# One new list of steps for a delta rule and a multiplicative FFN on one core: loads on SyncE's queue, clearing in steps of its own, and copies that name their engine

## The chip, the cores and the metric

The kernel runs on one core of a Trainium2 chip. The metric is device microseconds of one execution; lower is better. TensorE (PE) multiplies, VectorE (DVE), ScalarE (ACT) and GpSimd (POOL) work on vectors, and SyncE (SP) issues transfers. Each engine takes its instructions in order.

## The reference

```python
# deltanet: B, H, S, D = 4, 8, 768, 48
k_n = k / (norm(k, axis=-1) + 1e-06)
state = zeros((B, H, D, D))
for t in range(S):
    y[:, :, t] = einsum('bhd,bhde->bhe', q[:, :, t], state)
    v_old = einsum('bhde,bhd->bhe', state, k_n[:, :, t])
    state += beta[:, :, t] * outer(k_n[:, :, t], v[:, :, t] - v_old)
# multiplicative FFN on x = y as (3072, 384); d_ff = 1024
out = (((x @ w1) * (x @ w2)) @ w3) @ w_out
```

The queries, keys, values and beta are float32; the weights come as float64, so the kernel makes float32 of them.

## The kernel before

The sequence is cut into 12 chunks of 64 tokens, and the recurrence is brought to matrix products per chunk, with the inverse of a triangular matrix for each batch, head and chunk. Two chunks make a pair: `V0` is the inverse for chunks 0 and 1, and so on to `V5`. The FFN is folded: `w3 @ w_out` is made once (`w34`, eight folds), so that the FFN is `((x @ w1) * (x @ w2)) @ w34`. From the second pair of chunks on, the large products are done with fewer multiplications and sums on the vector engines.

The order of the whole program is written out in a string, `ORDER`, of step names. Every name stands for a Python generator; each time the name comes up, the generator runs to its next `yield`, and what it issues goes to the queues of the engines. At the end every engine is held to this order. The names that matter here:

- `P0` to `P7` are pieces of w_out, `P8` to `P23` of w3, `P24` to `P35` of w1 and w2. A piece (`piece`) has four steps: its transfer into one of five buffers `raw` (SP), two passes on ACT (L799, L802), a shift of bits on DVE (L804), and a sum on POOL (L806), which frees the buffer. The sixth transfer waits for the first sum.
- `k`, `q`, `v` and `p` load keys, queries, values, and keys and queries in another layout (`perm`, `spare`). `k0` and `q0` are issued from ACT's queue, the others from SP's.
- `K0`, `Q0`, `K1`, `Q1` (`by_tensor`, L352) turn the keys and queries of the first two chunks on PE; four copies follow, two of the keys' on DVE (L364), the others on ACT (L362). `d2` and on turn them on DVE instead (L339).
- `t0` to `t15` turn pieces of w3 on PE (L841), with a copy on ACT (L844). Piece P(8 + n) belongs to t(n). `f0` to `f7` are the folds (L855), in two halves, with a copy on ACT (L862).
- `g` makes squares of the keys (POOL, L285) and their sums (DVE, L287), and copies them across partitions (ACT, L274 and L276). `N` makes the norms of a pair in 15 small instructions of DVE, and copies across again.
- `s` is the scores of a chunk (PE, L383 and L389), with U made on DVE (L395) and P copied on ACT and masked on POOL. `u` copies U into columns (ACT, POOL, ACT).
- `V` is the inverse: POOL clears its start, DVE turns the columns (L466), ACT copies the start into PSUM (L475), 31 steps of two DVE instructions follow (L484, L489), and DVE turns the result back (L503). For the pairs from the third on, transfers take the place of some copies.
- `e` is the corner of the inverse for a chunk: copies from the result (ACT, POOL, ACT), a turning on DVE (L559), and two rounds of products on PE (L576) with copies on ACT.
- `c` is the chain through the state (L647), `y` the output of a chunk (L746). `a`, `b`, `h`, `i`, `j` are the FFN's first products (L875, L994), `S` and `G` sums for them, `o` and `x` the last products (L1104) and the results.

Before the first step, `padded` lets POOL clear `TT`, `perm`, `spare`, `x_room`, the ends of the four key tiles, and four more tiles (L198).

Of the kernel before, what the change touches and what calls it, by code (L numbers as in the profile page):

```python
# [39 lines left out]
V0 P0 k0 beta P18 P13 P0 P18 P0 P0 P11 g0 P13 K0 P18 K0 P11 P18 P10 P13 P13 q0 P3 P3 P11 g0 beta  # L40
beta K0 K0 K0 k1 K1 P10 P11 P12 P3 P12 g0 g0 Q0 P10 g0 g0 g0 g0 g0 P8 Q0 Q0 Q0 K1 K1 K1 Q0 K1 P3
N0 P9 k2 P8 P8 P10 s0 P8 N0 g1 s0 s0 s0 s0 s0 s0 u0 q1 P2 Q1 P9 p2 P2 P12 P12 P9 Q1 g1 Q1 Q1 P2
u0 g1 Q1 d2 d2 u0 P5 P1 t0 t0 t5 t5 P9 t2 t2 P4 P6 s1 s1 P5 P5 P2 s1 P1 s1 s1 s1 u1 g1 P1 u1 u1
t4 V0 V0 P5 V0 V0 P4 t10 P7 P4 t3 t3 V0 V0 P1 f1 P6 P6 t4 V0 P7 V0 V0 t10 t1 P14 P7 P4 V0 f0 V0
P6 P16 P16 V0 V0 P7 t1 s0 P19 P19 P19 P19 V0 f1 P17 k3 p2 v1 V0 V0 P14 P14 P14 V0 f2 P17 f2 f0 V0
f2 P15 v0 P20 f1 t11 f0 P17 P17 f5 V0 V0 P16 t11 P16 t8 P15 V1 V0 t8 f5 t9 V0 V0 t6 P15 V0 n0 n0
f5 V0 V0 V0 V0 t9 P20 P20 V0 t6 P22 P22 P22 f4 P23 P23 V0 f4 f4 P21 P21 P15 t7 t7 V0 s1 V0 V0 V0
V0 g1 d2 d2 P22 f3 f3 P24 P20 g1 g1 p3 g1 P26 p3 P30 e0 e0 e0 t12 t14 e1 e1 g1 f3 e0 e0 d3 d3 N1
s2 s2 s2 P23 P23 t12 e0 f6 e0 p4 s2 P24 e1 e1 t14 s2 e0 P24 s2 P25 c0 P26 f7 u2 P30 P24 c0 e1 e1
P21 P21 d3 d3 y0 y0 P26 P26 P31 t15 t13 s3 s3 s3 s3 s3 s3 t13 c0 n1 n1 P32 t15 u2 u2 u3 c0 P30 f7  # L50
e1 P25 P25 P31 P31 P27 c1 c1 u3 u3 f6 e1 c1 V1 V1 V1 y0 P31 f6 f7 P25 P27 V1 V1 V1 V1 P30 b1 c1
N1 b1 v2 P32 V1 V1 P27 V1 s1 y1 y1 b2 V1 d4 V1 V1 P28 P29 P32 b2 P27 V2 V1 V1 V1 y1 b3 V1 V1 P28
P28 b0 P32 c1 b2 b2 b3 b1 b1 b0 P29 P29 b0 P29 a03 a03 a02 V1 b0 V1 d4 V1 V1 a01 V1 P28 V1 V1 a02
V1 P35 a01 a00 a00 n2 n2 a04 a04 b7 P33 P33 a05 a05 P34 P34 a01 a07 b7 V1 b4 b5 V1 V1 V1 V1 k4
a01 a07 k5 b5 b3 g2 b4 V1 V1 P35 V1 V1 g2 c1 e2 e2 e2 e2 a06 a06 g2 e3 e3 e3 b3 g2 g2 a00 a02 a02
p4 v3 d4 d4 p5 a00 e2 P34 c2 c2 e2 P34 e2 b6 P35 P35 e2 c2 c2 e3 a03 g2 g2 P33 b6 y2 g2 P33 g2 d5
d5 p5 c2 c2 y2 a04 e3 s4 N2 e3 s4 a03 s4 b6 b6 s4 s4 s4 s4 T e3 T T d5 n3 d5 a04 e3 b4 b4 b7 s5
n3 k6 g3 u4 s5 s5 s5 s5 s5 s5 b5 b7 b5 a05 T c3 c3 a06 a05 a06 u5 V2 p6 g3 a07 a07 c3 c3 g3 S0 S0
S0 V2 g3 V2 V2 N2 oD0 y3 y3 V2 V2 W oA0 S0 S0 V2 V2 S0 S0 S0 c3 v5 n5 V2 V2 S0 S0 S0 S0 V2 v4 oB0
V2 V2 V2 xA0 V2 V2 xB0 V2 V2 oA0 S0 S0 S0 n4 oB0 xA0 d6 y3 k7 xA0 V2 n4 oC0 V2 V2 V2 a10 xB0 S0  # L60
V2 V2 xC0 G1 V2 xD0 a10 a10 V2 oC0 a10 a10 d6 xC0 xC0 xC0 xD0 V2 V2 i10 V2 h10 c3 c4 V2 V2 j10 V2
V2 V2 a10 h10 i10 a12 V2 V2 h10 W W a12 p6 V2 a12 a12 j12 e4 g3 g3 h10 c4 a12 h10 a12 h12 d6 d6
s5 i12 e4 e4 e4 i10 h12 h12 g3 g3 p7 g3 e4 e4 h12 N3 s4 h12 a11 a11 a11 s6 s6 i12 i12 e5 c4 j11
s6 c4 y4 y4 c4 e5 d7 d7 h11 c4 c5 a11 p7 e5 s6 a11 a11 h11 i11 i11 n5 c5 d7 d7 N3 a13 h11 h11 e5
W e5 s7 e5 a13 s7 s7 s7 s7 s7 s7 a13 a13 s6 s6 c5 i11 k8 u7 u6 g4 g4 g4 S1 V3 V3 c5 p8 h11 s6 g4
h13 a13 j13 a13 i13 h13 i13 i13 S1 h13 V3 h13 h13 V3 V3 y5 V3 V3 V3 V3 V3 V3 d8 V3 V3 V3 y5 oC1
oA1 S1 oD1 S1 S1 V3 V3 S1 xA1 c5 oA1 xA1 oB1 v6 y5 v7 a20 a20 V3 xA1 V3 V3 V3 d8 G2 V3 V3 xB1 n6
V3 V3 V3 V3 oB1 xB1 xC1 S1 j20 k9 V3 xD1 V3 V3 V3 V3 S1 oC1 a20 a20 p8 xC1 V3 xC1 h20 V3 xD1 xC1
# [27 lines left out]
def kernel(  # L96
# [13 lines left out]
    B, H, S, D = q.shape  # L110
    P = 128
# [65 lines left out]


# [15 lines left out]
    def padded(name, shape, n, start=0):  # L194
        res = []
        for i in range(n):
            t = persist.tile(shape, FP32, name=f"{name}{i}")
            pool.memset(t[:, start:] if start else t[:], 0.0)  # L198
# [146 lines left out]
    def by_tensor(m, i, src):  # L345
        KQ = KQs[m] if m in KQs else new_KQ(m)
        ps = [bank([P, NR, NP, C]) for z in range(2)]
        for r in range(NR):
            for h in range(H):
                for z in range(2):  # L350
                    x = half(z if i else (z + h) % 2)
                    pe.matmul(  # L352
                        ps[z][feat(h % 2), r, h // 2, :], lhsT=src[x, r, h, :],
                        rhs=ident[x, x], start=True, stop=True,
                    )
        yield
        for z in range(2):
            for e in range(2):
                o = KQ[feat(e), NR * z : NR * z + NR, :, i, :].rearrange("p b a t -> p (b a) t")
                x = ps[z][feat(e)].rearrange("p r a t -> p (r a) t")  # L360
                if i or e:
                    act.copy(out=o, in_=x)  # L362
                else:
                    dve.tensor_copy(out=o, in_=x)  # L364
                yield
# [471 lines left out]
    def transpose_w3(jc, hf):  # L837
        ps = bank([P, 4, P])
        w3 = w3s.pop((jc, hf))
# [4 lines left out]
        act.copy(out=w3Ts[jc, hf][:], in_=ps[:].rearrange("p a b -> p (a b)"))  # L844
# [4 lines left out]
    def fold(jc):  # L849
        ps = bank([P, CW])  # L850
        first = not folded
# [10 lines left out]
        act.copy(out=w34[:, jc, :], in_=ps[:, 0:DM])  # L862
# [352 lines left out]
    for m in range(2):  # L1215
        parts[f"q{m}"] = lambda m=m: load_q(m, act.dma_start if m == 0 else sync.dma_start)
# [77 lines left out]
```

## Time and profile before

| | us |
|---|---|
| Median of 3 runs | 555.05 (553.54 to 555.67) |
| Profiled execution, its own time | 554.45 |
| Profiled execution, span | 552.7 |
| PE busy in the span | 521.4 |
| DVE, ACT, POOL busy | 362.1, 187.6, 253.6 |
| Mean granted clock of PE | 0.994 |

A row of a timeline has its start and the time it lasted in us, the engine, the line of the kernel, the operation, out<-in, and the count; in brackets stands the idle time ahead of it and what ended that. SPq and ACTq are the queues in which an engine issues transfers. A row of waits has the engine and line that waited, what it waited for, the total in us, how often, and the longest.

### The profile page before, as it was taken

The numbers are of one execution on the slowest core, as the hardware profiler recorded it, in microseconds if no ns is written. First come the engines' busy times: TensorE is split into PE (matmuls) and PEld (weight loads), VectorE is DVE, ScalarE is ACT, GpSimd is POOL, SyncE is SP. The second block draws the span as 40 slices with busy tenths as digits, with TensorE's granted clock in tenths as the row PEclk, the third lists the DMA queues.
The fourth block names the chain that finished last, engine by engine and source line by source line (L and its number), as shares of the span: only waits on it lengthen the run. The fifth ranks groups of instructions, "written<-read, shape, count | busy, mean of one in ns | idle before, by whom it ended". The sixth has DMA issues, their size and how long they took to land.

```text
span 552.7 us, 19818 instructions
## 1 busy us (share of the span) xinstructions
PE 521.4 (94%) x8540; PEld 447.8 (81%) x8540; DVE 362.1 (66%) x814; ACT 187.6 (34%) x393; POOL 253.6 (46%) x278
## 2 busy tenths in 40 slices
PE   3686999999999999999999999999999999999997
PEld 2563666688878988889987889988899888998897
DVE  2757877798767878569967579858587654123332
ACT  4788388955633012422022430123231121300000
POOL 8466555453569960365343255510492212342141
PEclk9997999999999999999999999999999999999999
DMA  8987987669356345454553564253601220020001
GB/s 251 203 223 189 199 188 141 120 159 150 55 90 127 80 106 80 61 101 81 114 98 61 79 121 86 86 83 43 125 16 44 62 51 5 9 66 1 0 1 57
DMA packets 197687, 52.64 MB, mean 95 GB/s; under 512 B 185344, under 2 KB 191488, under 8 KB 197600
## 3 DMA queue, kind: packets, MB, share of 16 engines
q1 hardware_dynamic: 193408, 50.59, 44.6%
q10 hardware_dynamic: 4192, 0.79, 0.9%
q8 instruction: 67, 1.10, 0.8%
q14 instruction: 20, 0.16, 0.1%
HBM read 41.25 MB, written 8.91 MB: 91 GB/s over the span
## 4 chain that ended last, share of the span: by engine, by line
PE 80%; DMA 6%; ACT 5%; DVE 4%; SPq 2%; issue 1%; DVEq 0%; ACTq 0%
PE ps_f L994 33%; PE ps_f L1104 19%; PE ps_f L855 7%; PE ps_w L647 6%; PE ps_f L875 6%; PE ps_w L746 4%; PE ps_w L576 2%; DMA X<-in_q_dram 2%; PE ps_w L383 2%; PE ps_w L389 1%; DMA raw<-in_moe_w_dram 1%; DMA ktok<-in_k_dram 1%; SPq L253 1%; DVE KQ L339 1%; ACT raw L802 1%
## 5 line engine op out<-in xcount | busy, mean ns | idle before, releaser
L1002 DVE TENSOR_TENSOR ab<-ab,ps_f 128x512 f32<-128x512 f32 x80 | 54.5, 682 | 57.3 <-PE ps_f L994 56.8
L1075 POOL TENSOR_TENSOR ab<-ab 128x512 f32<-128x512 f32 (+1 forms) x56 | 61.3, 1116 | 41.8 <-PE ps_f L1104 25.4
L994 PE MATMUL ps_f<-xT,w1s 128*128 128x256 f32 x320 | 78.5, 382 | 0.0
L1041 POOL TENSOR_TENSOR ab<-ab,late 128x512 f32<-128x512 f32 x19 | 24.1, 1271 | 107.0 <-DVE ab L1002 106.3
L994 PEld LDWEIGHTS ps_f<-xT,w1s 128*128 128x128 f32 x320 | 59.9, 190 | 7.9
L1104 PE MATMUL ps_f<-w,ab 128*128 128x192 f32 x376 | 65.5, 328 | 0.0
L1104 PEld LDWEIGHTS ps_f<-w,ab 128*128 128x128 f32 x376 | 61.3, 190 | 1.3 <-issue 0.5
L409 POOL TENSOR_TENSOR PT<-PT,smask 128x512 f32<-128x512 f32 x20 | 25.5, 1277 | 54.9 <-ACT PT L407 54.9
L855 PE MATMUL ps_f<-w2s,w3T 128*128 128x384 f32 x128 | 45.9, 510 | 4.9 <-ACT w3T L844 4.9
L1104 PE MATMUL ps_f<-room,ab 128*128 128x192 f32 x272 | 47.2, 328 | 0.0
L500 DVE TENSOR_TENSOR ps_w<-ps_w,tb 128x31 f32<-128x31 f32 (+15 forms) x124 | 43.3, 349 | 4.2
L767 ACT COPY xT<-ps_w 48x256 f32<-48x256 f32 x96 | 30.4, 365 | 44.8 <-PE ps_w L746 44.3
L1104 PEld LDWEIGHTS ps_f<-room,ab 128*128 128x128 f32 x272 | 44.3, 190 | 0.6 <-issue 0.3
L495 DVE TENSOR_TENSOR tb<-ps_w,Ub 128x31 f32<-128x31 f32 (+15 forms) x124 | 41.9, 338 | 3.6 <-ACT ps_w L475 0.3
L1010 ACT COPY ab<-ps_f 128x512 f32<-128x512 f32 x20 | 11.7, 586 | 95.1 <-PE ps_f L994 95.0
L994 PE MATMUL ps_f<-xT,room 128*128 128x256 f32 x160 | 41.3, 385 | 0.3 <-DVE ab L1002 0.2
L855 PEld LDWEIGHTS ps_f<-w2s,w3T 128*128 128x128 f32 x128 | 24.4, 198 | 20.8 <-issue 6.6
L994 PE MATMUL ps_f<-xT,w2s 128*128 128x256 f32 x160 | 40.1, 381 | 0.0
L994 PE MATMUL ps_f<-x_room,w2s 128*128 128x256 f32 x160 | 38.9, 386 | 0.0
L994 PEld LDWEIGHTS ps_f<-xT,room 128*128 128x128 f32 x160 | 29.5, 190 | 5.5 <-DVE ab L1002 1.1
L994 PEld LDWEIGHTS ps_f<-x_room,w2s 128*128 128x128 f32 x160 | 29.5, 190 | 5.1 <-DVE late L1002 1.0
L994 PEld LDWEIGHTS ps_f<-xT,w2s 128*128 128x128 f32 x160 | 30.1, 190 | 4.0
(143 smaller groups left out, 977.2 us busy)
## 6 DMA issues: line engine op xcount, KB each, us to landing
raw<-in_moe_w_dram SPq DMA_DIRECT2D x16, 512.0 KB, 6.7
vtok<-in_v_dram SPq DMA_DIRECT2D x24, 192.0 KB, 4.4
raw<-in_moe_w_dram SPq DMA_DIRECT2D x24, 192.0 KB, 4.9
out_dram<-osb SPq DMA_DIRECT2D x46, 96.0 KB, 1.7
ktok<-in_k_dram SPq DMA_DIRECT2D x44, 96.0 KB, 3.4
raw<-in_moe_w_out_dram SPq DMA_DIRECT2D x8, 384.0 KB, 4.5
perm<-in_k_dram SPq DMA_DIRECT2D x40, 64.0 KB, 2.8
perm<-in_q_dram SPq DMA_DIRECT2D x32, 64.0 KB, 2.8
```

Source lines behind the costliest of these rows:

```text
L409: pool.tensor_tensor(out=PT, in0=PT, in1=smask[:].unsqueeze(1).to_broadcast([P, H, C]), op=ALU.mult)
L495: dve.tensor_tensor(out=tv, in0=V[:, 0 : s + 1, s : s + 1].to_broadcast([P, s + 1, n]), in1=U[:, s, s + 1 : BS].unsqueeze(1).to_broadcast( ...
L500: dve.tensor_tensor(out=o, in0=o, in1=tv, op=ALU.subtract)
L647: pe.matmul(out(ps, r, h, z), lhsT=lhs(r, h, z), rhs=rhs(r, h, z), start=True, stop=True,)
L767: act.copy(out=xT[f, p:NP:2, b : b + NR, cc, :].rearrange("p a r t -> p r a t"), in_=pyv[f, z, b : b + NR],)
L855: pe.matmul(ps[:, 0:DM], lhsT=w3Ts[jc, kc // 4][:, kc % 4 * P : kc % 4 * P + P], rhs=wo[:, kc], start=(i == 0), stop=(i == KF - 1),)
L875: pe.matmul(ps[:].rearrange("p b c t -> p b (c t)"), lhsT=w[:, m, js], rhs=x[:, m, :, c0:c1].rearrange("p b c t -> p b (c t)"), start=(m = ...
L994: pe.matmul(acc[name][:, n * i : n * i + n], lhsT=ws[b][:, P * i : P * i + P], rhs=xs[x], start=new and k == 0 and i == 0, stop=k == len(t ...
L1002: dve.tensor_tensor(out=o_, in0=x, in1=acc[name], op=ALU.add)
L1041: eng.tensor_tensor(out=Z1, in0=Z1, in1=late, op=ALU.mult)
L1075: pool.tensor_tensor(out=o_, in0=x_, in1=y_, op=op)
L1104: pe.matmul(ps[b][:, b, :], lhsT=block(u, HF * f + i, z)[:, P * b : P * b + P], rhs=ws_[w][:, i], start=first and i == 0 and (b == 0 or n ...
```

## The change

1. `k0` and `q0` are issued from SP's queue, as the other loads are.
2. `padded` only notes what is to be cleared. Two new steps clear: `zd` on DVE (half of `TT`, those half columns of `perm` and `spare` that the loads leave out), and `zp` on POOL (the rest), one tile each time the name comes up.
3. A mark `'` behind a step's name swaps the engine of the copy that it issues: with it, a copy that was ACT's is DVE's and the other way. It holds for the copies of `K`, `Q`, `t` and `f`. A number behind `+` lets a step issue products that nobody reads; the list has none.
4. `ORDER` is a new list. It names the same steps, with the three novelties, in another order throughout.

In the new list, the first transfers are P12, P10, k0, q0, P11, beta, k1, P8, P18, P0, P13, q1; in the old one they are P0, k0 (ACT), beta, P18, P13, P11, P10, q0 (ACT), P3, k1.

```diff
 ORDER = """
-V0 P0 k0 beta P18 P13 P0 P18 P0 P0 P11 g0 P13 K0 P18 K0 P11 P18 P10 P13 P13 q0 P3 P3 P11 g0 beta
-beta K0 K0 K0 k1 K1 P10 P11 P12 P3 P12 g0 g0 Q0 P10 g0 g0 g0 g0 g0 P8 Q0 Q0 Q0 K1 K1 K1 Q0 K1 P3
...
-f5 V0 V0 V0 V0 t9 P20 P20 V0 t6 P22 P22 P22 f4 P23 P23 V0 f4 f4 P21 P21 P15 t7 t7 V0 s1 V0 V0 V0
-V0 g1 d2 d2 P22 f3 f3 P24 P20 g1 g1 p3 g1 P26 p3 P30 e0 e0 e0 t12 t14 e1 e1 g1 f3 e0 e0 d3 d3 N1
...
+P12 zp zp zp P10 P10 P12 zd P12 P12 P10 k0 K0 g0 g0 K0' g0 q0 V0 P10 K0' Q0 Q0' K0' zd P11 beta k1
+beta K0 P11 beta g0 P8 Q0' Q0 Q0 P8 g0 P11 g0 zp g0 g0 K1 P8 P18 P11 K1 g0 K1 K1' K1 P18 N0 P0 P0
+P13 t3 P8 s0 P0 P18 P0 P18 zp q1 P5 P9 k2 t2 P13 s0 s0 t2 P13 Q1 P5 zd Q1' Q1 t3 P3 P2 P13 s0 s0 s0
+s0 u0 u0 Q1' Q1' P5 p2 t4 P9 u0 P3 P7 P5 g1 t4' P9 P9 s1 P1 s1 s1 s1 s1 s1 u1 u1 u1 t0 t0' P3 t1 P2
+g1 t5 P2 P3 P2 V0 V0 V0 V0 P7 t1 d2 V0 P1 t5 P6 P7 P6 V0 d2 P1 t10 P7 t10 P4 P16 V0 V0 V0 V0 P6 V0
...
+g1 f4 P15 t7 t6 t7 f3 f3 v1 v0 N1 P21 e1 e0 P22 e0 n0 e0 e0 e0 d2 s2 P23 p3 e1 P29 P21 P21 e0 s2 t14
...
 """
...
+    def put(eng, out, in_):
+
+        on_act = (eng is act) != bool(other)
+        (act.copy if on_act else dve.tensor_copy)(out=out, in_=in_)
...
+    zeros = []
+
+    def padded(name, shape, n, start=0, where=None, eng=pool):
...
-            pool.memset(t[:, start:] if start else t[:], 0.0)
+            zeros.append((eng, where(t) if where else t[:, start:] if start else t[:]))
...
+    def zero(part):
+        for eng, t in zeros:
+            if (eng is dve) == part:
+                eng.memset(t, 0.0)
+                yield
...
-                if i or e:
-                    act.copy(out=o, in_=x)
-                else:
-                    dve.tensor_copy(out=o, in_=x)
+                put(act if i or e else dve, o, x)
...
+    parts["zd"] = lambda: zero(True)
+    parts["zp"] = lambda: zero(False)
...
-        parts[f"k{m}"] = lambda m=m: load_k(m, act.dma_start if m == 0 else sync.dma_start)
+        parts[f"k{m}"] = lambda m=m: load_k(m)
...
-        parts[f"q{m}"] = lambda m=m: load_q(m, act.dma_start if m == 0 else sync.dma_start)
+        parts[f"q{m}"] = lambda m=m: load_q(m)
...
     def step(name):
 
+        name, _, n = name.partition("+")
+        other[:] = name[len(name.rstrip("'")):]
+        name = name.rstrip("'")
+        unread[0] = int(n or 0)
```

More of the change, by code (lines that the diff above doesn't have):

```diff
@@ L51 @@
[L51 to L56, printed above, removed]
@@ new lines @@
+oC1 oA1 V3 V3 V3 V3 V3 V3 V3 V3 S1 S1 n6 s6 xA1 y5 p8 oB1 oD1 V3 V3 V3 V3 S1 S1 oA1 n6 s7 V3 V3 V3
+xB1 V3 V3 V3 k8 V3 V3 y5 oB1 d8 xA1 y5 V3 d8 V3 V3 G2 xA1 xB1 V3 V3 xC1 c5 a20 a20 k9 xC1 a20 j20 V3
+v7 V3 V3 a20 V3 xD1 S1 S1 oC1 xC1 p8 V3 V3 n7 a20 a20 V3 V3 V3 V3 V3 h20 h20 i20 c5 e6 h20 h20 i20
+a22 a22 a22 h20 a22 h22 a22 a22 i22 i20 xD1 a21 d8 e6 e6 h22 c6 h22 g4 g4 d8 e6 e6 N3 e6 c6 h22 j22
+xC1 e7 a21 a21 g4 g4 g4 g4 e7 i22 i22 g4 c6 e7 a21 a21 a21 c6 h21 y6 p9 e7 c6 j21 h22 h21 d9 g4 d9
@@ new lines @@
+c6 y6 n7 V4 g4 N4 v8 n8 i21 h21 p9 s8 h21 s8 s8 s8 s8 s8 s8 i21 a23 a23 a23 c7 u8 d9 d9 p10 a23 s9
+i23 h21 c7 s9 s9 s9 s9 s9 s9 i21 s9 u9 V4 e7 j23 a23 h23 a23 h23 V4 e7 V4 c7 c7 h23 y7 h23 i23 i23
+h23 S2 S2 y7 V4 V4 V4 V4 V4 V4 V4 d10 V4 V4 oD2 oA2 c7 d10 xA2 oA2 xA2 S2 S2 V4 S2 V4 V4 V4 s8 V4 V4
+V4 S2 S2 oB2 xB2 y7 V4 oC2 oB2 V4 c7 V4 xB2 xC2 G3 v9 S2 n8 a30 a30 a30 V4 xA2 k10 V4 oC2 j30 xD2
+k11 xC2 xD2 a30 V4 V4 xC2 a30 V4 V4 V4 V4 V4 a30 h30 h30 xC2 i30 n9 V4 V4 V4 V4 V4 a32 h30 c8 p10
@@ L92 @@
+c11 c11 xB4 c11 y10 oD4 y10 y11 y11 y11 oA4 S4 S4 S4 S4 oB4 oC4 xB4 xD4 xC4 a50 xC4 xD4 G5 oC4 a50
+a50 a50 xA4 j50 xA4 xC4 xC4 h50 a50 i50 a50 h50 i50 h50 h50 a52 a52 a52 h52 i50 h50 a52 a52 a52 h52
+j52 h52 h52 i52 i52 a51 a51 a51 h51 i52 h52 a51 a51 a51 h51 j51 h51 h51 h51 i51 i51 i51 a53 a53 a53
+a53 h53 a53 j53 a53 h53 h53 h53 h53 i53 i53 i53 S5 S5 o5 x5 o5 o5 S5 o5 x5 x5 S5 o5 x5 S5 S5 o5 x5
+x5 x5 S5 x5 x5 x5 S5 o5 x5 x5 x5 x5
 """
@@ L176, with fill @@
     pe, dve, act, pool, sync = nc.tensor, nc.vector, nc.scalar, nc.gpsimd, nc.sync
+    other = []
+    unread = [0]
+    def fill(ps):
+        for _ in range(unread[0]):
+            pe.matmul(
+                ps, lhsT=ident[:], rhs=ident[:].unsqueeze(1).to_broadcast([P, 4, P]),
+                start=True, stop=True,
+            )
+    def put(eng, out, in_):
+        on_act = (eng is act) != bool(other)
+        (act.copy if on_act else dve.tensor_copy)(out=out, in_=in_)
     small.tile([P, 40], FP32, tag="pad", name="pad", bufs=1)
@@ L191 @@
         pool.tensor_copy(out=smask[half(z), :], in_=strict[half(z), half(z)])
-    def padded(name, shape, n, start=0):
+    zeros = []
+    def padded(name, shape, n, start=0, where=None, eng=pool):
         res = []
@@ L197, in padded @@
             t = persist.tile(shape, FP32, name=f"{name}{i}")
-            pool.memset(t[:, start:] if start else t[:], 0.0)
+            zeros.append((eng, where(t) if where else t[:, start:] if start else t[:]))
             res.append(t)
         return res
-    TTx = padded("TT", [P, 2, NR, H, C], 1)[0]
-    TTs = [TTx[:, i] for i in range(2)]
-    perm = padded("perm", [P, B, NP, 2, BS], 1)[0]
-    spare, x_room = (padded(x, [P, n], 1)[0] for x, n in (("spare", 1024), ("x_room", 512)))
+    def zero(part):
[3 more added lines that the diff above has]
+                yield
+    TTx = padded("TT", [P, 2, NR, H, C], 1, where=lambda t: t[:, :, :, :, 0:BS], eng=dve)[0]
+    TTs = [TTx[:, i] for i in range(2)]
+    perm = padded(
+        "perm", [P, B, NP, 2, BS], 1, where=lambda t: t[:, :, :, :, D - BS :], eng=dve
+    )[0]
+    spare = padded(
+        "spare", [P, 1024], 1, eng=dve,
+        where=lambda t: t[:].rearrange("p (g d) -> p g d", d=BS)[:, :, D - BS :],
+    )[0]
+    x_room = padded("x_room", [P, 512], 1)[0]
     def perms(m):
@@ L347, in by_tensor @@
         ps = [bank([P, NR, NP, C]) for z in range(2)]
+        fill(ps[0].rearrange("p r a t -> p (r a t)"))
         for r in range(NR):
@@ L377, in scores @@
             ps = two_banks()
+            fill(ps[:, 0])
             for h in range(H):
@@ L838, in transpose_w3 @@
         ps = bank([P, 4, P])
+        fill(ps[:].rearrange("p x f -> p (x f)"))
         w3 = w3s.pop((jc, hf))
@@ L843, in transpose_w3 @@
         w3Ts[jc, hf] = slab("w3T")
-        act.copy(out=w3Ts[jc, hf][:], in_=ps[:].rearrange("p a b -> p (a b)"))
+        put(act, w3Ts[jc, hf][:], ps[:].rearrange("p a b -> p (a b)"))
         yield
@@ L850, in fold @@
         ps = bank([P, CW])
+        fill(ps[:])
         first = not folded
@@ L861, in fold @@
         yield
-        act.copy(out=w34[:, jc, :], in_=ps[:, 0:DM])
+        put(act, w34[:, jc, :], ps[:, 0:DM])
         yield
```

72 lines of the change are left out of this document (30 added, 42 removed).

## The prediction

> **What bounds the kernel now.** I read the page first, then the stretches, then who waits for whom on TensorE (PE), then the queues of the opening in order of time.
>
> ```profile
> span 552.7 us, 19818 instructions
> PE 521.4 (94%) x8540; PEld 447.8 (81%) x8540; DVE 362.1 (66%) x814; ACT 187.6 (34%) x393; POOL 253.6 (46%) x278
> ```
>
> PE is busy for 521.4 of 552.7 us, so only 31.3 us can be had without taking matmuls away. The stretches (columns: window, length, busy time of PE, weight loads, DVE, ACT, POOL; clock; DMA share; GB/s) say where they lie:
>
> ```profile
> 0.00:48.50 48.50, 26.19 (x496) 21.15 (x496) 26.40 (x60) 35.27 (x64) 33.68 (x48) 0.96 0.83 214
> 48.50:81.60 33.10, 33.09 (x116) 20.37 (x116) 25.41 (x66) 20.05 (x37) 18.30 (x19) 0.95 0.90 204
> 81.60:540.00 458.40, 453.19 (x7876) 397.57 (x7875) 307.22 (x683) 132.27 (x293) 200.75 (x211) 1.00 0.40 76
> 540.00:552.70 12.70, 8.98 (x56) 8.68 (x54) 3.12 (x7) 0.00 (x0) 0.88 (x1) 1.00 0.19 62
> ```
>
> 22.3 us of PE's idle time lie ahead of 48.5, none in the next 33 us, 5.2 in the long middle, 3.7 at the end. The change can win in the opening; behind it, it can mostly lose. PE's waits in the opening:
>
> ```profile
> PE ps_f L352 <- DMA ktok<-in_k_dram: 12.4, 4, 4.7
> PE ps_f L855 <- ACT w3T L844: 4.9, 2, 4.7
> ```
>
> First it waits for keys, later for a copy on ScalarE (ACT). The fold (L855) needs all of w_out (pieces P0 to P7), and each piece takes two passes on ACT, one on DVE, one on POOL. After the folds PE meets the corner of the first inverse (L576), which needs the 31 steps on VectorE:
>
> ```profile
> 45.86 1.62 PE L855 MATMUL ps_f<-w2s,w3T 128*128 128x384 f32 x2 [4.67 <-ACT w3T L844]
> 48.51 14.67 PE L855 MATMUL ps_f<-w2s,w3T 128*128 128x384 f32 x40 [0.18 <-ACT w3T L844]
> 63.46 2.75 PE L855 MATMUL ps_f<-w2s,w3T 128*128 128x384 f32 x8
> ...
> 80.69 1.04 PE L841 MATMUL ps_f<-ident,w 128*128 128x128 f32 x8
> 81.66 0.74 PE L576 MATMUL ps_w<-T,U 33*33 33x32 f32 x63
> ```
>
> So 81.66 is the time to forecast: the order on PE is almost the same work before and after that corner in both lists, and what follows is dense.
>
> **The change part by part.**
>
> *Keys and queries on SyncE (SP).* The issues of k0 and q0 leave ACT's queue; SP now sends two w3 pieces (1.05 MB), then k0, q0, a third piece, beta, k1.
>
> ```profile
> 8.42 2.47 PE L352 MATMUL ps_f<-ident,ktok 64*48 64x64 f32 x62 [3.27 <-DMA ktok<-in_k_dram]
> 10.74 2.71 SPq L225 DMA_DIRECT2D ktok<-in_k_dram  x4
> 18.55 1.83 PE L352 MATMUL ps_f<-ident,ktok 64*48 64x64 f32 x57 [1.04 <-DMA ktok<-in_k_dram]
> ```
>
> k0 was all there at 8.42. I put it at 8.5: about as many bytes stand ahead of it (one w_out piece, beta and the first w3 piece then, two w3 pieces now). Bounds: 7.5, and 11.9 if the 1.05 MB go wholly first (the rival below). k1 waits for SP's earlier transfers and goes out from about 8.2 on; from issue to the last block of its turning took 18.55 - 10.74 = 7.8 us, so 16.0 instead of 18.55. q1 is sent behind a piece that waits for POOL's second sum, at about 15.3 (the old list sends it behind k2); its copies come late enough in ACT's queue not to hold it. ACT wins the time of issuing, but it would only have waited for its first piece then: worth 0.
>
> *Clearing in own steps.* POOL cleared everything ahead of its first sum:
>
> ```profile
> 2.51 1.80 POOL L198 MEMSET TT<- 128x2048 f32 x1
> 9.32 1.02 POOL L806 TENSOR_TENSOR w2s<-w2s,raw 128x384 uint32<-128x384 uint32 x1
> 18.72 1.61 POOL L285 TENSOR_TENSOR sq<-ktok 128x384 f32<-128x384 f32 x2 [2.15 <-DVE w L804]
> ```
>
> Now it clears x_room and two pads first and sums from about 9.2, when the first piece has been through ACT: no gain there. DVE clears half of TT while it has nothing else (0 on the path, at most 1.80), and a quarter of that area twice more, ahead of beta's copy and of the second query's (0.2 to 0.9 each; ACT has 2 us queued beside them). Taken as 0.
>
> *ACT's queue, up to the first inverse.* 16.0, the squares of k1 (1.61), one reduction (0.54, a group below) and 0.1 give the crossing copies of the norms at 18.3 instead of 21.66.
>
> ```profile
> 21.66 0.19 ACT L274 COPY ss<-ss 128x16 f32<-128x16 f32 x1
> 25.69 0.67 ACT L799 ACTIVATE w<-raw 128x512 f32<-128x512 f32 x1
> 26.82 0.19 ACT L274 COPY wt<-wt 128x16 f32<-128x16 f32 x1
> 40.84 2.15 ACT L446 COPY columns<-U 96x512 f32<-96x512 f32 x2
> 43.02 1.21 ACT L475 COPY ps_w<-Vb 128x512 f32<-128x512 f32 x2
> 46.97 0.58 ACT L799 ACTIVATE w2s<-raw 128x384 f32<-128x384 f32 x1
> 47.87 0.59 ACT L844 COPY w3T<-ps_f 128x512 f32<-128x512 f32 x1
> ```
>
> Prices: a copy 0.6 (half of 1.21), a w3 piece 1.15 (25.69 to 26.82), a w_out piece 0.95 (46.97 to 47.87), a columns copy 1.07. From the crossing (0.6) to the end of the copies into V (1.21) ACT had 2 w3 and 3 w_out pieces, 10 copies of keys and queries, 3 of w3, 3 masks, 4 columns and a crossing of weights (0.6): 21.5, and took 22.6 (21.66 to 44.23). Now it has 3 and 4 pieces, 4 copies of keys and queries, 2 of w3, 3 masks, 4 columns: 3.45 + 3.8 + 5.4 + 4.3 with the two ends 1.8, or 18.7. With 1.0 for waits the copies into V end at 38.0 instead of 44.23. The copies that DVE takes over (0.67 each, the group below) lie beside this: DVE is busy 26.40 of 48.5 us. What would be late next is P2 or the columns on POOL, both some 1 us ahead of their use.
>
> *The first inverse.* DVE's groups between 44.4 and 75.6 (count, busy, mean ns, idle before), and three groups of the opening:
>
> ```profile
> L489 DVE TENSOR_TENSOR ps_w<-ps_w,tb 128x31 f32<-128x31 f32 (+15 forms) x31 | 10.8, 349 | 1.1
> L484 DVE TENSOR_TENSOR tb<-ps_w,Ub 128x31 f32<-128x31 f32 (+15 forms) x31 | 10.5, 339 | 0.8
> L804 DVE TENSOR_SCALAR w<-w 128x512 uint32<-128x512 uint32 x7 | 3.0, 422 | 5.3 <-ACT w L799 5.3
> L804 DVE TENSOR_SCALAR w2s<-w2s 128x384 uint32<-128x384 uint32 x3 | 1.1, 357 | 0.0
> ...
> L364 DVE COPY KQ<-ps_f 48x512 f32<-48x512 f32 x4 | 2.6, 674 | 1.6 <-PE ps_f L352 1.6
> L287 DVE TENSOR_REDUCE ss<-sq 128x8 f32<-128x384 f32 x6 | 3.3, 544 | 1.2 <-POOL sq L285 1.2
> L339 DVE STREAM_TRANSPOSE KQ<-perm 128x512 f32<-128x512 f32 x2 | 1.3, 690 | 2.8 <-DMA perm<-in_k_dram 2.8
> ...
> 75.68 1.25 DVE L503 STREAM_TRANSPOSE Ub<-ps_w 128x1024 f32<-128x1024 f32 x1
> 79.92 0.71 DVE L559 STREAM_TRANSPOSE T<-TT 128x512 f32<-128x512 f32 x1 [0.91 <-ACT TT L549]
> 81.74 0.14 DVE L294 TENSOR_SCALAR seed<-ss 128x32 uint32<-128x32 uint32 x1
> 85.01 0.19 DVE L318 TENSOR_TENSOR wt<-wt,beta_tok 128x32 f32<-128x32 f32 x1
> ```
>
> From the copies' end (44.23) to the turning back (75.68) are 31.4 us: 5.3 of waiting for ACT's weights, 26.1 of steps and ten shifts of pieces. The new list has ten shifts there too, and besides three turnings of keys or queries (0.69) and three reductions (0.54): 3.7. With 1.2 of waiting: 38.0 + 26.1 + 3.7 + 1.2 = 69.0 instead of 75.68.
>
> *The corner, where the list loses.* From the turning back (75.68) to the turning of the corner (79.92) passed 4.2 us, taken by copies on ACT and POOL. The new list has the norms of the second pair (81.74 to 85.20, 3.5 us of DVE) and a shift ahead of that turning; they fill the 3.0 us in which DVE waited and cost 0.9 more. 69.0 + 4.2 + 0.9 = 74.1, turned (0.71) at 74.8, and half a microsecond to PE: 75.3 instead of 81.66, **-6.4**.
>
> *Is PE there by then?* ACT has four w_out pieces (3.8) and three copies of w3 (1.8) after 38.0, and POOL sums the last (1.02): 44.6 for all of w_out. Nine half folds of 2.6 (row 63.46, 8 matmuls) and six turnings of w3 (0.48, half of 80.69 to 81.66) bring 70.9, and the slow clock at their start, as in the 14.67 for five halves, 1.7 more. So PE comes at 72.6 and waits 2.7 us for the corner, perhaps longer, and that may cost clock:
>
> ```profile
> 44.00:45.00 1.00, 0.00 (x0) 0.88 0.35 82
> 45.00:51.00 6.00, 4.96 (x10) 0.50 0.89 294
> 51.00:52.00 1.00, 1.00 (x3) 0.71 1.05 315
> ```
>
> The clock fell to half in the fourth microsecond of the wait that began at 41.2 and came back 5.7 us after PE began again: at most 2.9 us lost. The Trainium skill, "TensorE: Matmul & The Clock Gate" (What's actually happening), says that an idle window of about 3.4 us halves the clock, which this agrees with. By that rule a wait of 2.7 us would keep the clock, and the sum would be 1.0 less. I take a third of the loss, **+1.0**, since the wait is less sure than its distance from the fourth microsecond; bounds 0 and 2.9.
>
> *The rest.* V1, V2 and so on are spread over DVE much as before, and the end on PE is the same. New are pairs with little between: the second chain step follows the first's state with only one block of scores between them. **+0.5** from the 5.2 us of idle middle; bounds -3 and +5.
>
> Sum against the profiled execution's own 554.45 (span 552.7 and 1.75 around it): 554.45 - 6.4 + 1.0 + 0.5 = 549.55. The median of the runs shown, 555.05, is 0.6 above that execution; I give **550.0**.
>
> **The rivals.** *One ring.* k0 goes behind 1.05 MB, which at the 294 to 315 GB/s above take 3.4 us: 11.9, and keys, squares, columns and V0 all come 3.4 later, 553.4, no change. The Trainium skill, "DMA: Bandwidth & Descriptors" (Issuing engines are not separate DMA queues; Queues, rings and completion order), speaks against this change: SP and ACT each have a ring on the same engines, served in turn, and each ring starts in its order. For it: the 1.05 MB now stand ahead on k0's own ring. Against: with a ring to itself k0's last part came only at 8.42, after PE had stood 3.27 us for it, so sharing had already cost it most of this.
>
> *The inverse waits for weights* (slower). In the new list six w3 shifts stand inside V0, and ACT's passes for them stand behind copies that wait for folds on PE. The old inverse stood four times, 5.3 in all; if each of the six stands for 1.8, that is 10.8 instead of 1.2: 559.6. It decides from 9 us in all (550.0 + 7.8 passes the old time by 0.5%). For it: DMA is 0.90 busy in 48.5 to 81.6, and the old inverse did stand. Against: by the sum above ACT is through with w_out 4 us sooner.
>
> *More than that.* No clock lost, PE's 5.2 us of idle middle cut by 3: 545.2.
>
> That the copies do not move can be left out: the changed program's queues have them where the list says.
>
> **How the numbers follow.** Forecast 0.46 (547 to 552.2), more 0.14, one ring 0.19, slower 0.21. About 0.5%, 2.8 us, is what a measurement of this kernel can tell: faster 0.60, same 0.19, slower 0.21. The range leaves out the lowest tenth and half of the slower case: 544 to 559.
>
> **What would show it.** Right: PE's first L352 at about 8.5; ACT's copies into V ending near 38; 31 steps from 38 to 69; corner on PE near 75 with a wait of about 3 us for DVE. Wrong: k0 near 12; shifts in V0 with waits of over 1.5 each; a fold that waits for w_out past 47; or more than 8 us of idle PE from the corner to 540.

## The result, and the profile after

| | before | after |
|---|---|---|
| Median, us | 554.88 (553.54 to 555.67) | 568.55 (566.89 to 570.31) |
| Profiled execution, span | 552.7 | 567.4 |
| PE busy in the span | 521.4 | 526.2 |
| First corner on PE begins at | 81.66 | 79.47 |
| From there to the end | 471.0 | 487.9 |

The new kernel is slower: ratio 1.0249, 95% interval 1.0211 to 1.0288. The forecast of 550.0 was wrong by 18.6 us. Single executions fall now and then into a slower state of the chip; ratios leave these out, medians do not, so the two can differ a little.

The page of the new kernel, and its stretches with the cuts at its own corner (columns as before):

```profile
span 567.4 us, 19834 instructions
PE 526.2 (93%) x8540; PEld 450.0 (79%) x8540; DVE 369.6 (65%) x825; ACT 183.3 (32%) x385; POOL 251.3 (44%) x275
```

```profile
0.00:48.50 48.50, 30.96 (x514) 23.81 (x514) 31.70 (x74) 34.60 (x61) 30.31 (x42) 0.82 0.90 226
48.50:79.50 31.00, 26.01 (x100) 15.68 (x99) 29.25 (x73) 15.74 (x29) 15.95 (x19) 1.00 0.91 199
79.50:554.70 475.20, 460.32 (x7879) 401.88 (x7880) 305.50 (x673) 132.94 (x295) 204.28 (x215) 0.99 0.39 73
...
80.00:90.00 10.00, 10.00 (x277) 7.80 (x265) 5.96 (x12) 7.44 (x14) 6.80 (x9) 0.66 0.73 130
```

Behind the corner nearly the same number of matmuls (7879 against 7876) takes 475.2 us instead of 458.4: PE stands idle for 14.9 us instead of 5.2, and is busy for 7.1 us longer, at a mean clock of 0.99 instead of 1.00. A part of that is in the last row: a mean clock of 0.66 in 10 us means 6.8 us at half speed, or 3.4 us lost. The waits name no single culprit, as PE's list shows (waited for; total, times, longest):

```profile
PE ps_w L605 <- DVE T L588: 4.6, 2, 4.3
PE ps_w L676 <- issue: 3.8, 3, 2.0
PE ps_w L775 <- issue: 3.2, 3, 2.4
...
PE ps_f L1025 <- DVE room L1165: 2.0, 1, 2.0
PE ps_f L1025 <- DVE osb L1165: 1.9, 1, 1.9
```

(Line numbers of the new kernel are about 30 above the old ones: L605 was L576, the corner; L676 was L647, the chain; L775 was L746, the outputs; L1025 was L994.) The opening is as forecast, and its last step is not. The timeline of the new kernel, the rows that answer to the prediction's steps:

```profile
8.55 2.43 PE L383 MATMUL ps_f<-ident,ktok 64*48 64x64 f32 x61 [0.66 <-DMA ktok<-in_k_dram]
16.81 2.17 PE L383 MATMUL ps_f<-ident,ktok 64*48 64x64 f32 x62 [1.77 <-DMA ktok<-in_k_dram]
19.59 0.19 ACT L304 COPY ss<-ss 128x16 f32<-128x16 f32 x1
38.28 1.20 ACT L504 COPY ps_w<-Vb 128x512 f32<-128x512 f32 x2
47.66 1.01 POOL L835 TENSOR_TENSOR w2s<-w2s,raw 128x384 uint32<-128x384 uint32 x1 [0.35 <-ACT w L828]
69.93 1.25 DVE L532 STREAM_TRANSPOSE Ub<-ps_w 128x1024 f32<-128x1024 f32 x1
78.71 0.70 DVE L588 STREAM_TRANSPOSE T<-TT 128x512 f32<-128x512 f32 x1
79.47 0.73 PE L605 MATMUL ps_w<-T,U 33*33 33x32 f32 x62 [4.33 <-DVE T L588]
```

Down to the turning back at 69.93 (forecast 69.0, old 75.68) nearly all of the gain is there. The turning of the corner comes at 78.71, not at 74.1. Between them stand the norms, VectorE beside GpSimd:

```profile
71.84 1.17 DVE L334 TENSOR_TENSOR nt<-nt,seed 128x32 f32<-128x32 f32 x1
73.04 1.12 DVE L336 SCALAR_TENSOR_TENSOR nr<-nt,seed 128x32 f32<-128x32 f32 x1
74.20 0.87 DVE L331 SCALAR_TENSOR_TENSOR nt<-ss,nr 128x32 f32<-128x32 f32 x1
...
76.00 1.06 DVE L331 SCALAR_TENSOR_TENSOR nt<-ss,nr 128x32 f32<-128x32 f32 x1
77.09 0.19 DVE L334 TENSOR_TENSOR nt<-nt,nr 128x32 f32<-128x32 f32 x1
...
71.62 1.33 POOL L835 TENSOR_TENSOR w<-w,raw 128x512 uint32<-128x512 uint32 x1 [5.06 <-ACT w3T L192]
73.02 1.09 POOL L578 COPY TT<-Ub 32x512 f32<-32x512 f32 x1
74.19 0.83 POOL L662 TENSOR_TENSOR vtok<-vtok,n 128x384 f32<-128x384 f32 x1
...
75.98 1.03 POOL L578 COPY TT<-Ub 32x512 f32<-32x512 f32 x1
```

Each long row ends within 0.1 us of the end of the row of GpSimd beside it (73.01 and 72.95, 74.16 and 74.11, 75.07 and 75.02, 77.06 and 77.01), and with GpSimd at rest the same instruction takes 0.19 us. The norms took 7.4 us (71.41 to 78.79) instead of 3.5.

### The profile page after: what moved, and what is told of

It reads as the page before. It is cut to its first block, busy times and chain, and to the rows that moved or that the text cites. A ratio compares the mean times of both kernels' runs of the same rounds, so it can differ in the third digit from the quotient of the medians.

```text
span 567.4 us, 19834 instructions
## 1 busy us (share of the span) xinstructions
PE 526.2 (93%) x8540; PEld 450.0 (79%) x8540; DVE 369.6 (65%) x825; ACT 183.3 (32%) x385; POOL 251.3 (44%) x275
## 4 chain that ended last, share of the span: by engine, by line
PE 72%; DVE 10%; SPq 6%; DMA 5%; issue 4%; POOL 2%; ACT 0%; POOLq 0%; DVEq 0%
PE ps_f L1025 35%; PE ps_f L1135 15%; PE ps_w L676 5%; PE ps_w L775 4%; PE ps_w L605 3%; PE ps_f L906 3%; PE ps_f L886 2%; PE ps_w L412 2%; PE ps_w L418 2%; DMA ktok<-in_k_dram 1%; SPq L266 1%; DVE tb L524 1%; DVE ps_w L529 1%; DVE ps_w L518 1%; SPq L820 1%
## 5 line engine op out<-in xcount | busy, mean ns | idle before, releaser
L1025 PE MATMUL ps_f<-xT,w1s 128*128 128x256 f32 x320 | 80.1, 387 | 0.0
L1025 PEld LDWEIGHTS ps_f<-xT,w1s 128*128 128x128 f32 x320 | 60.5, 192 | 8.4
L1025 PE MATMUL ps_f<-xT,room 128*128 128x256 f32 x160 | 41.5, 386 | 3.9 <-DVE room L1165 2.0
L1025 PE MATMUL ps_f<-xT,w2s 128*128 128x256 f32 x160 | 40.2, 382 | 0.0
L1025 PE MATMUL ps_f<-x_room,w2s 128*128 128x256 f32 x160 | 38.9, 386 | 0.0
L1025 PEld LDWEIGHTS ps_f<-xT,room 128*128 128x128 f32 x160 | 29.4, 190 | 9.5 <-DVE osb L1165 2.4
L1025 PEld LDWEIGHTS ps_f<-x_room,w2s 128*128 128x128 f32 x160 | 29.5, 190 | 5.3 <-DVE late L1033 1.2
L1025 PEld LDWEIGHTS ps_f<-xT,w2s 128*128 128x128 f32 x160 | 30.0, 190 | 4.3 <-DVE ab L1033 0.3
```

Source lines behind the costliest of these rows:

```text
L1025: pe.matmul(acc[name][:, n * i : n * i + n], lhsT=ws[b][:, P * i : P * i + P], rhs=xs[x], start=new and k == 0 and i == 0, stop=k == len(t ...
```

## The experiments

Theories at the start: A, the drawn-out norms hold the corner and that is the loss; C, the opening is worth what was forecast and the order behind the corner loses it; D, the opening itself costs; later G, SyncE's queue sets the pace behind the corner. A line of a diff here is a stretch of the list; the rest of the list stays.

**Where in the list the loss lies.** Three lists put together from the two. The step that each cut names is the first of the other list's order; no step is lost or doubled.

```diff
 new_head:   new list to the step before N1, then all other steps in the old order
 new_to_s0:  new list to the step before the first S0 (about 150 us), then the old order
 new_rest:   the opening's steps in the old order, old clearing, loads and engines of copies, then the new list from N1
```

> The new list up to the first corner (to the step before the norms of the second pair), then all remaining steps in the old list's order; clearing, loads and engines of the copies as in the new kernel. Theory C (the opening is worth what was forecast, and the new order behind the corner loses it all and more: PE stands 7 us more behind 150 and 7 us more between 70 and 150): 548 to 554, so at or under the old kernel's time. Theory D (the opening itself costs: its clock at half from 15 to 35 us, later weights, transfers in other order): over 560, though the rest is the old one.

> The new list up to the first of the sums for the last products of the first pair (about 150 us), then all remaining steps in the old list's order. If the loss is made between the corner and there (4.3 us of PE idle at the corner, 2.6 behind it, and the slow clock of 80 to 90), the time stays at 565 to 568; if it is made behind (7.1 us more of PE idle from 150 to the end), 560 to 562; that both count is my expectation, 561.

> The reverse: the same steps as in the new list's opening, but in the old list's order, with the old clearing, loads and engines of the copies, and then the new list from the norms of the second pair on. Theory C: the loss stays, 565 to 572. Theory D: it goes, under 558.

Measured: new_head 555.53, ratio 1.0015 (0.9980 to 1.0050); new_to_s0 563.11, 1.0129 (1.0079 to 1.0178); new_rest 573.23, 1.0314 (1.0277 to 1.0351). So the loss lies wholly behind the corner: the new opening with the old order behind it takes the old time. By the medians 7.6 us lie between the corner and the first S0 (563.1 - 555.5) and 5.4 behind it (568.55 - 563.11); by the ratios it is 1.1% and 1.2%, so about half on each side. D falls. C is right on the loss, but not on the gain: new_head should have been faster, and is not.

**The corner.** One step of the list moved, and then two ways further.

```diff
 n1_later:       -N1 P21 e1 e0 P22 e0 n0 e0 e0 e0 d2 s2
                 +P21 e1 e0 P22 e0 n0 e0 e0 e0 N1 d2 s2
 corner_clear:   +P21 e1 e0 P22 e0 n0 e0 e0 e0 d2 s2 N1
 corner_and_x6:  corner_clear, and x6_first (below)
```

> The new kernel with one step moved: the fifteen small instructions that make the norms of the second pair stand behind the turning and the first products of the first corner, not ahead of them. Theory A (the norms, drawn out to 7.4 us by GpSimd working beside them, hold the corner): T is turned near 74 instead of 78.7, PE's wait of 4.6 us at that corner falls under 1, the half clock of 80 to 90 us goes, and the time falls by 4 to 7 us, to 562 to 564. Theory B (the corner only moves what the steps behind it lose anyway, since they wait for chains of small dependent steps): the corner is as early as in A, but the time falls by less than 2 us, 567 or more.

> The new kernel with the norms of the second pair behind chunk 2's first scores on PE, so behind the corner's turning and behind the last turning of chunk 2's keys and queries too: in n1_later PE only took its 4.2 us of waiting one step further, to those scores. Theory J (the loss between the corner and 150 us is this one wait and the half clock behind it, 4.3 + 3.4 us): no wait over 1.5 us between 70 and 85 us, no half clock there, and 5 to 7 us less than the new kernel's 566 to 569, so 560 to 562. Theory K (behind the corner PE would stand anyway, by the weights and by chain steps with little between them): 565 to 568.

> The same, and the scaling of X in chunk 6's chain ahead of the sum that waits, as in x6_first. If the places are independent, the 2.6 us (4 in the profile) that x6_first brought come off the time of corner_clear: theory J 557 to 559, theory K 562 to 565.

Measured: n1_later 571.35, 1.0277 (1.0221 to 1.0332); corner_clear 566.21, 1.0105 (1.0049 to 1.0161), its executions from 558.0 to 567.9; corner_and_x6 563.22, 1.0150 (1.0113 to 1.0186). PE's longest wait between 72 and 112 us, of n1_later and then of corner_and_x6:

```profile
PE ps_w L414 <- DVE KQ L371: 4.2, 1, 4.2
```

```profile
PE ps_w L607 <- DVE PT L444: 3.2, 1, 3.2
```

The corner begins at 75.70 and 74.78 on PE (75.52 in corner_clear), as forecast for the new kernel (75.3). In n1_later the time does not fall: the wait of 4.3 us goes on to the next step that stands behind the norms in VectorE's queue, chunk 2's keys (4.2). With the norms further back it goes on to the masks that free its bank (3.2). The granted clock hides a part of what such a move brings. The stretch from 72 to 112 us in the profiled executions of the new kernel and then of n1_later:

```profile
72.00:112.00 40.00, 31.47 (x944) 23.46 (x943) 26.85 (x53) 27.90 (x50) 21.01 (x23) 0.91 0.60 116
```

```profile
72.00:112.00 40.00, 32.70 (x816) 24.58 (x814) 21.95 (x45) 25.63 (x44) 18.82 (x21) 0.79 0.63 117
```

A mean clock of 0.91 in 40 us is 3.6 us lost, 0.79 is 8.4. In corner_clear and corner_and_x6 it is 0.96 and 0.87. So theory A falls as it was put: the corner is early in n1_later, and the 4 to 7 us are not gained. What the norms' place is worth stays open between J and K. For J: the ratio of corner_clear, 1.0105, lies clear below the new kernel's (1.0249, and 1.0205 in after_again below); but it rests on three of six executions (558.04, 559.57 and 565.75), and the profile is of one of 566.66 that is not among them. For K: corner_and_x6, the same with the other place mended too, has 1.0150, as x6_first has without it (1.0154).

**Why the opening brings nothing.** In new_head the corner on PE began at 77.93, 3.7 us before the old kernel's, and the first products with w1 at 107.98, the same as in the old kernel. In new_head and then in head_no_p3 (below) they begin so:

```profile
107.98 0.70 PE L908 MATMUL ps_f<-xT,w1s 128*128 128x256 f32 x2 [0.60 <-DMA xT<-xT]
```

```profile
105.20 1.56 PE L911 MATMUL ps_f<-xT,w1s 128*128 128x256 f32 x6
```

The profiled execution of new_head took 558.4 us, 2.9 above the median, so a little of what its trace loses is its own. PE's waits of new_head between 72 and 112:

```profile
PE ps_w L414 <- DVE PT L444: 1.9, 1, 1.9
PE ps_w L607 <- DVE T L590: 1.3, 1, 1.3
...
PE ps_f L908 <- POOL PT L440: 1.2, 1, 1.2
```

SyncE issues all that time, in new_head and then in the old kernel (timeline of its queue):

```profile
78.81 5.52 SPq L285 DMA_DIRECT2D spare<-in_q_dram  x8
84.42 1.83 SPq L822 DMA_DIRECT2D raw<-in_moe_w_dram  x4
86.35 5.26 SPq L285 DMA_DIRECT2D perm<-in_k_dram  x8
91.73 11.15 SPq L822 DMA_DIRECT2D raw<-in_moe_w_dram  x16
```

```profile
79.67 4.15 SPq L253 DMA_DIRECT2D spare<-in_q_dram  x8
83.92 2.57 SPq L791 DMA_DIRECT2D raw<-in_moe_w_dram  x4
86.59 5.13 SPq L253 DMA_DIRECT2D perm<-in_k_dram  x8
91.83 10.14 SPq L791 DMA_DIRECT2D raw<-in_moe_w_dram  x16
```

Both queues are full, and from 86 us on they are at the same place at the same time. The clock counts beside them: from 82 to 112 us it is 0.91 in new_head, 1.00 in the old kernel and 0.99 in head_no_p3, so 2.7 us of full clock are lost in this execution of new_head. Four kernels on that; p3 is the load of chunk 3's keys and queries, p4 of chunk 4's:

```diff
 before_no_p3, head_no_p3:          -the 16 transfers of p3 (old kernel; new_head)
 head_p3_pool, head_p3_act:         -sync.dma_start  +pool.dma_start / act.dma_start for p3 (new_head)
 head_p4_later, before_p4_later:    first p4 (8 transfers) moved behind the transfer of P27 (new_head; old kernel)
```

> The old kernel without the 16 transfers that bring chunk 3's keys and queries in the layout for VectorE (left out: chunk 3 is computed with chunk 2's keys and queries). SyncE's queue issues without a pause from 75 to 102 us in the old kernel, and these 16 take 6.8 us of it; the pieces of w1 and w2 stand behind them. Theory G (behind the first corner the pace is set by SyncE's queue, at the same time in both lists): the old kernel stands for little there (idle 1.6 us from 82 to 112), so it gains 1 to 2 us, 553 to 554. Theory H (the queue has nothing to do with it): no change, 555.

> The same 16 transfers left out of the kernel with the new opening and the old order behind it, which had its corner 3.8 us earlier and had lost that again by 108 us, where PE begins on w1. Theory G: the pieces of w1 and w2 come about 6 us earlier, the new opening's 3.8 us come through, and the time is 549 to 551, 3 to 4 us under the old kernel with the same cut. Theory H: 555, as with the transfers.

> The kernel with the new opening and the old order behind it, all its transfers made, but the 16 that bring chunk 3's keys and queries are issued from GpSimd's queue and not from SyncE's. Theory G (SyncE's queue sets the pace behind the corner): most of the 3.8 us that leaving them out gave, 552 to 553, and so the first version under the old kernel; GpSimd pays 16 issues between 78 and 92 us, where it is busy for 4 to 5 of 10 us, and if one takes over 0.5 us the sums of the weights' pieces come later and it is 555 or more. Theory H (it was the transfers themselves, on the 16 DMA engines, not the queue that issues them): 555 to 556.

> The same with these 16 transfers on ScalarE's queue. ScalarE is busy for 8.8 of the 10 us from 70 to 80 and 6.3 from 80 to 90 in that kernel; four issues took it 2.8 us in the old kernel, so 16 take 8 to 11 us in which its copies for the corner wait. Theory G and H both expect 557 to 563, slower than with SyncE's queue; if ScalarE has the room, G expects 552.

> The kernel with the new opening and the old order behind it, with one step moved: the eight transfers of chunk 4's keys in the layout for VectorE (5.3 us of SyncE's queue, from 86.4 us) go behind four pieces of w1 and w2, which stood behind them; nothing is left out. Theory G (SyncE's queue sets the pace behind the corner): the pieces come up to 5 us earlier and most of what leaving out the 16 transfers gave comes, 552 to 553, a version under the old kernel. Theory H, or if chunk 4's keys are then late for VectorE: 555 or more.

> The same step moved in the old kernel. By theory G no change, 555, as without the 16 transfers (554.6), since PE has its work there until its own corner comes 3.8 us later.

Measured: before_no_p3 554.62, 0.9995 (0.9971 to 1.0019); head_no_p3 551.71, 0.9959 (0.9933 to 0.9986), 3.8 us under new_head and 2.9 under before_no_p3 by the medians; the intervals overlap a little, and 551.71 is just outside the 549 to 551 of theory G. There products with w1 begin at 105.20 instead of 107.98. So without these loads a part of the opening's lead seems to come through, while the old kernel, whose PE has its folds to do meanwhile, gains nothing by the same cut. The traces do not show how the lead reaches the end: the profiled execution of head_no_p3 (555.1 us) is the slowest of its ten and has lost it again there.

The other four brought nothing. head_p3_pool took 561.32 (1.0125, 1.0098 to 1.0152) and head_p3_act, expected at 557 to 563, 564.58 (1.0181, 1.0150 to 1.0212): the list has p3 ahead of the corner's copies, so on GpSimd's queue the issues stand in front of them (timeline), and PE waits for the corner:

```profile
73.07 5.30 POOL L285 DMA_DIRECT2D perm<-in_k_dram  x8
79.24 5.13 POOL L285 DMA_DIRECT2D spare<-in_q_dram  x8 [0.87 <-DMA raw<-in_moe_w_dram]
84.42 2.03 POOL L580 COPY TT<-Ub 32x512 f32<-32x512 f32 x2
```

```profile
PE ps_w L607 <- DVE T L590: 10.5, 1, 10.5
```

head_p4_later took 558.21 (1.0071, 1.0045 to 1.0096) and before_p4_later 558.07 (1.0061, 1.0034 to 1.0087), 3 us more in both. The moved transfers now stand in front of those that complete the first outputs, and PE waits for them (head_p4_later):

```profile
PE ps_f L908 <- DMA xT<-xT: 3.1, 1, 3.1
```

This shows that the order of SyncE's queue decides who waits there; it does not show the gain that G promised. The pieces of w1 and w2 are issued some 4 us sooner in head_p4_later, and the products with w1 begin no sooner (108.70): they wait for these outputs (`xT`), not for the weights. SyncE issues them from 103.47 in new_head, from 104.40 in head_p4_later and from 96.77 in head_no_p3. That fits the queue; whether head_no_p3 gained by it alone, by the 16 DMA engines or by VectorE's shorter waits stays open. It computes with other keys, so it is no version to use; none that computes all of it beat the old kernel.

**Single places behind the corner.** Chunk 6's output on PE waits for X. In the new kernel's timeline VectorE has X behind a sum that itself waits for PE:

```profile
305.64 0.69 DVE L1033 TENSOR_TENSOR ab<-ab,ps_f 128x512 f32<-128x512 f32 x1 [3.14 <-PE ps_f L1025]
306.24 0.95 DVE L716 TENSOR_TENSOR X<-ps_w,wt 128x768 f32<-128x768 f32 x1
```

```diff
 x6_first:    -c6 e7 a21 a21 a21 c6 h21 y6
              +c6 e7 c6 a21 a21 a21 h21 y6
 two_places:  x6_first, and
              -oB1 d8 xA1 y5 V3 d8 V3 V3 G2 xA1 xB1
              +oB1 xB1 d8 xA1 y5 V3 d8 V3 V3 G2 xA1
 after_again: the new kernel, unchanged
```

> The new kernel with two steps of its list moved. The scaling of X in chunk 6's chain (VectorE) goes five steps forward, so that it no longer stands behind a sum (L1033) that waits 3.1 us for a product; PE's wait of 2.5 us at 304.7 to 307.2, the 0.96 us ahead of it and the half clock from 310 to 314 hang on it. The second sum of the second pair's result B goes ten steps forward, ahead of three steps of the inverse; PE's wait of 2.0 us at 274 hangs on it. Theory E (the loss behind the first corner is made of single places where one step of VectorE stands in the wrong order in its queue, and each is lost once): 2.5 + 1.0 + 1.7 + 2.0 = 7.2 us less, 561 to 563. Theory F (VectorE and the transfers are behind as a whole, and a wait that is taken away comes back at the next step): 566 or more.

> The new kernel again, as the measure for the next one on the same chip: 567 to 570.

> The new kernel with one step moved: the scaling of X in chunk 6's chain stands ahead of the sum that waits for a product. In the execution profiled before with this and a second step moved, PE's wait of 2.5 us ahead of chunk 6's output was gone, and the output of chunk 7 began 6.5 us sooner than in the new kernel (330.7 instead of 337.2), of which 2.2 were there already ahead of chunk 6. Theory E: 4 us less than the new kernel beside it (2.5 of the wait and 1.7 of half clock). Theory F: less than 1.5 us less.

Measured: two_places 566.59, 1.0194 (1.0138 to 1.0251), too wide to tell. On one chip after_again 566.58, 1.0205 (1.0170 to 1.0241), and x6_first 563.96, 1.0154 (1.0120 to 1.0188): 2.6 us less, between theories E (4) and F (under 1.5), with intervals that overlap a little; corner_and_x6 beside corner_clear shows no such gain. The place itself is clear in the traces. X runs at 302.13, and the stretch from 290 to 335 us, of after_again and then of x6_first:

```profile
290.00:335.00 45.00, 41.51 (x1030) 34.99 (x1032) 25.99 (x51) 12.83 (x30) 12.21 (x13) 0.96 0.48 81
```

```profile
290.00:335.00 45.00, 43.80 (x1145) 37.30 (x1145) 28.59 (x56) 13.25 (x32) 13.57 (x15) 1.00 0.50 86
```

With one step in another place PE stands 2.3 us less, the clock stays full, and 115 more matmuls get done. The second place of two_places gave nothing: PE's wait of 2.0 us for `room` became one of 1.7 at the next product.

**The loads alone.** One edit each, in the old list and back in the new one:

```diff
 loads_on_sp (old kernel):  -load_k(m, act.dma_start if m == 0 else sync.dma_start)  +load_k(m), and the same for load_q
 loads_back (new kernel):   -load_k(m)  +load_k(m, act.dma_start if m == 0 else sync.dma_start), and the same for load_q
```

> The old kernel with the loads of the first keys and queries on SyncE's queue, and nothing else changed: there one piece of w_out stands ahead of the first keys. If sharing the ring costs what I gave the rival, the first keys come at 8.4 + 2 and the time is 556 to 557; if the queue does not matter, 555; ScalarE, which no longer issues for 2.8 us, begins its first piece no sooner than that piece is there.

> The new kernel with the loads of the first keys and queries back on ScalarE's queue, where they are issued at once. In the old list the move to SyncE's cost 4 us (1.0072). If it costs that by itself, this one is 3 to 4 us faster than the new kernel, 563 to 565; if the cost lay in the old list, which has five pieces ahead of the queries, then the same, 566 to 569, since the new list sends both early and its loss lies behind the corner.

Measured: loads_on_sp 558.47, 1.0072 (1.0040 to 1.0104), 4 us slower; loads_back 579.66, 1.0435 (1.0398 to 1.0471), 11 to 13 us slower than the new kernel. Both misses of mine have the same cause, the place in an in-order queue (PE and then SyncE's queue in loads_on_sp, and ScalarE in loads_back):

```profile
6.25 2.38 PE L352 MATMUL ps_f<-ident,ktok 64*48 64x64 f32 x62 [1.01 <-DMA ktok<-in_k_dram]
```

```profile
10.25 5.22 SPq L791 DMA_DIRECT2D raw<-in_moe_w_out_dram  x1
15.52 2.71 SPq L225 DMA_DIRECT2D ktok<-in_k_dram  x4
```

```profile
8.00 0.66 ACT L828 ACTIVATE w<-raw 128x512 f32<-128x512 f32 x1 [5.92 <-DMA raw<-in_moe_w_dram]
8.02 0.69 ACTq L255 DMA_DIRECT2D ktok<-in_k_dram  x1
15.74 1.33 ACTq L266 DMA_DIRECT2D X<-in_q_dram  x2
```

In the old list the first keys are complete at 6.25 instead of 8.42, sooner and not 2 us later as expected; but the second keys go out at 15.52 instead of 10.74, behind a piece of w_out for which SyncE waits 4.2 us until a sum of GpSimd frees a buffer. In the new list ScalarE's passes over the first two pieces stand ahead of k0, so it is issued at 8.0 and q0 at 15.7, and all that follows is 12 us late. The move to SyncE belongs to the new list: it costs 4 us without it, and the list costs about 12 us more without the move.

## Why the prediction was wrong

- **Keys and queries: the times right, the reason only in part.** k0 was complete on PE at 8.55 (8.5 forecast), k1 at 16.81 (16.0). The rival of one ring, k0 at 11.9, did not come. But what stands ahead on the queue counts: behind one piece of w_out instead of two of w3 (loads_on_sp) k0 was complete at 6.25. So the new queue gained about what the two pieces cost, and that k0 came as late as before was in part luck. The Trainium skill, "DMA: Bandwidth & Descriptors" (Queues, rings and completion order), says that each ring starts in its order; 6.25 against 8.55 agrees with it.
- **ScalarE's queue and the inverse: right within 1.5 us.** Crossing 19.59 (18.3), copies into V done at 39.48 (38.0), the inverse 30.45 long (31.0). The rival in which the inverse waits for weights did not come.
- **"3.5 us of DVE" for the norms: wrong.** 7.4 us. I took the price from rows of the old kernel in which GpSimd was not beside them. With the norms behind it (n1_later) the corner began at 75.70, so this step cost some 4 us at the corner. The corner came 2.2 us earlier instead of 6.4.
- **Is PE there by then: off.** w_out was summed at 48.67 (44.6) and PE stood at the corner from 75.14 (72.6); the wait was 4.33 (2.7). The clock cost 3.4 us, outside my bounds of 0 and 2.9: the wait passed the fourth microsecond, and of the ten microseconds from 80 on 6.8 ran at half clock. A wait of 2.7 us would not have been safe either: in new_head one of 1.9 us (83.12 to 85.05) was followed by half clock from 86.3 to 89.75. The Trainium skill, "TensorE: Matmul & The Clock Gate" (What's actually happening), puts the return of the full clock after at least one busy window of about 3.4 us; here half clock lasted 6.8 us, in new_head 3.4.
- **"So 81.66 is the time to forecast ... what follows is dense": the premise that failed.** new_head had the corner 3.7 us earlier and the old time. n1_later, corner_clear and corner_and_x6 had it at about my own time, and took 1.0277, 1.0105 and 1.0150 of the old time, where my sum makes it about 0.99. My reading, which no run shows by itself, is that what follows was dense in the old kernel because its corner came as late as it did.
- **"The rest", +0.5 with bounds -3 and +5: the term that was mis-sized most.** 487.9 - 471.0 = 16.9, less the 3.4 of clock: 13.5, of which 9.7 are idle time of PE (14.9 - 5.2) and 1.7 half clock from 310 to 320 us (0.83 there). I priced a whole new order over 470 us from the idle time of the old one, and named the short distances between chain steps without counting them. The last of my own signs, over 8 us of idle PE from the corner on, is what came (14.9). One such place is shown in the traces (x6_first: 2.3 us of idle time; the 2.6 us by the medians are not clear of noise). The others behind the corner, a chain step behind one block of scores (PE L676, 3.8 us in all) and results on VectorE that free a bank late (L1165, 3.9), are read from the trace and not tried one by one; the half of the loss that lies before S0 is placed by the cuts, not explained. (The lowest rival's 545.2 is 545.1 by its own terms; nothing hangs on it.)

## What to carry to other kernels

A marker in the middle of a kernel is worth its lead only if what stands behind it can begin sooner: ask what feeds the work behind the marker, a queue or another engine, and whether that moves too. A new order can lose at any of its tight pairs, so walk the in-order queues and look for steps that stand behind a step which waits for another engine. Where a program is one list, a part of a change has no price of its own: the same two loads cost 4 us in one list and saved about 12 in the other.

## What the hardware showed that was not expected

Small VectorE instructions of 0.19 us took 0.87 to 1.17 us in the four rows above in which a GpSimd instruction ran beside them, to its end. The Trainium skill, "SBUF — State Buffer" (Who interferes with whom), says that a VectorE instruction with two inputs in SBUF contends with a GpSimd instruction that reads SBUF; these rows agree. And SyncE pays for issuing: 0.5 to 0.7 us for each of the small transfers above (5.52 for eight), so sixteen of them hold its queue for some 10 us.
